# Moving the shares of a triangular inverse in a chunked attention kernel: from nine to seventeen, one behind each dense half unit

## The chip, the cores and the metric

The kernel runs on one core of one Trainium2 chip. The metric is device microseconds of one launch. A core has a matrix engine (PE, with its weight loads PEld), three elementwise engines (DVE, ACT, POOL) that each work through their own list of instructions strictly in order, and SP, which here only starts DMAs. An instruction that needs another engine's result waits for a semaphore, and all that stands behind it on its own engine waits with it.

## What is computed

An attention recurrence over 768 steps, a dense two-layer network on its output, and a layer of eight experts of which each token uses one:

```python
for t in range(S):                                   # r,k,v,w,a,b: (4, 8, 768, 40)
    y[:, :, t] = einsum('bhd,bhde->bhe', r_t, state)
    Sa = einsum('bhde,bhe->bhd', state, a_t)
    state = state * w_t[:, :, None, :] - einsum('bhd,bhe->bhde', Sa, b_t) + einsum('bhd,bhe->bhde', v_t, k_t)
x = y.transpose(0, 2, 1, 3).reshape(3072, 320)
h = x @ w_in                                         # 320 -> 2048
x = maximum(0.01 * h, h) @ w_out                     # 2048 -> 320
e = argmax(x @ w_gate)                               # 8 experts
out = softmax(x @ w_gate)[e] * (relu(x @ w1[e]) @ w2[e])
```

## The kernel before, in words

**Attention in chunks.** The 768 steps are cut into 24 chunks of 32. Inside a chunk the recurrence becomes a triangular system. The kernel prepares a chunk some six chunks ahead in fifteen steps (`prep`): clamp and scans of the decay on DVE (L216, L224, L226, L239), two reciprocals (L232, L233), a product on POOL (L231, tile `AtI`), the keys on POOL and DVE (L242, L243, tile `KB`), small matmuls (L265), masks and copies, and at last DMAs, of which one kind collects the triangular blocks of four chunks in the tile `Pq` (L287). When four chunks are prepared, `inverse` turns `Pq` into the inverses of all their triangles at once. It has 62 steps: the first is a transpose on DVE from `Pq` into `Tinv` (L301); then come thirty pairs on POOL, a product into `itmp` (L309) and a sum into `Tinv` (L315), where each needs the one before; the last is a copy (L321) and a transpose (L323) on DVE into `TT`. The chunk's own steps s1 to s6 read `TT` in s2 (matmuls of L414), the first time in the chunk three after the one in which the inverse began. The inverses that this case is about begin in chunks 5, 9, 13 and 17 and have to be there in chunks 8, 12, 16 and 20.

**The dense layer runs beside it**, since the attention of an earlier pair of chunks is its input. It goes in units, each of 128 of the 2048 hidden columns for 256 tokens, and each unit in two half units. The first half issues layer 1: eight matmuls into a bank of PSUM (L722), then `g` on ACT (L726) and DVE (L727), then `gh`, the rounded `g`, on ACT (L728). The second half issues the six matmuls of layer 2 for the unit two back (L738; they need that unit's `gh`, and last its `gl`), and then `gl = g - gh` on POOL (L729) for this unit. There are two buffers of `g`, two PSUM banks for layer 1, and three of `gh` and `gl`. So ACT may only write `g` of a unit when POOL has made `gl` of the unit two before, and PE may only finish layer 2 of a unit when POOL has made its `gl`. Beside both stand the gate's logits of the tokens that are done (DVE L762, tile `junk`).

**The order is written by hand.** Each chunk plays a string of words: `H` is a half unit, `p` the next step of the preparation, `s1` to `s6` the chunk's own steps, `l2` and `l3` loads, and `w` a share of the inverse. A share takes the next steps of the open inverse, and how many follows from what is left and from how many shares are still to come up to the end of the third chunk:

```python
turns, k = order.count("w"), 0          # shares in this chunk's string
...
elif what == "w":
    for _ in range(-(-len(inv) // (turns * (4 - here % 4) - k))):
        inv.pop(0)()
    k += 1
```

`here` is the chunk's number. `len(inv)` is rounded up in the division, and in a chunk with number 4n+1 the divisor holds the chunk's full count of shares, also those that were played before the inverse was there. `STEP` is the string of chunks 5 to 18, `LATE` of 19 to 22, and both are at the top of the file. The preparation ends in chunk 17, so chunk 18 has the inverse and no preparation beside it.

Of the kernel before, what the change touches and what calls it, by code (L numbers as in the profile page):

```python
# [22 lines left out]
B, H, S, D = 4, 8, 768, 40  # L23
# [27 lines left out]
)  # L51
STEP = (
    "w s6a.-1 s1 s6b.-1 H H H s2 H H p w p p s3a s3x H l2.1 H p w p w p w p w p s3b p H H s4a p p s4b H p H w s5a s5b H p H p H w H w p H l3.1 "
)
LATE = (
    "s6a.-1 H H s1 H s6b.-1 w s2 H H w s3a s3x H w H s3b H l2.1 H H w H w s4a w s4b H s5a s5b H w H H w H l3.1 H w "
)
END = (
    "H H s1 H s2 w w H H H w H s6a.-1 s6b.-1 w s3x H H s3a w H s4a s4b H w H s5a s5b w l3.1 H H s3b H l2.1 H H w w H "
# [1417 lines left out]
```

## Time and profile before

| what | us |
|---|---|
| median of 3 runs (1087.32 to 1091.97) | 1090.9 |
| the profiled execution's own time | 1100.18 |
| its span | 1098.4 |
| PE busy | 929.3 |
| DVE busy | 807.6 |
| ACT busy | 531.3 |
| POOL busy | 512.3 |

The profiled execution is 9.3 us above the median of the runs. Its span is the time from its first to its last instruction, and 1.8 us lie around it. The busy times are sums over the whole program; what an engine does in one chunk is seen only in a window of that chunk. In the rows below a chunk is taken from its first matmul of s1 (L399) to the next chunk's.

### The profile page before, as it was taken

What the parts mean: (1) busy time and instruction counts of PE and PEld (TensorE: products, weight loads), DVE (VectorE), ACT (ScalarE), POOL (GpSimd) and SP (SyncE); (2) the same over time, 40 slices, a digit from 0 to 9 for tenths busy, and PEclk for the clock granted to TensorE, in tenths of its full rate; (3) what the DMA queues carried; (4) which work ended last, traced back from release to release, by engine and by line L of the source; (5) the groups of instructions that cost most, each with busy time, mean ns of one, the idle gap of its engine ahead of it and who ended that gap; (6) DMA issues with size and microseconds to landing.
All of it is one profiled execution on the core that took longest, in us unless ns stands there. A gap on an engine that the chain in (4) does not pass through costs nothing.

```text
span 1098.4 us, 40672 instructions
## 1 busy us (share of the span) xinstructions
PE 929.3 (85%) x16854; PEld 871.4 (79%) x16854; DVE 807.6 (74%) x1900; ACT 531.3 (48%) x1316; POOL 512.3 (47%) x690
## 2 busy tenths in 40 slices
PE   2265778878799888889889998999999799999995
PEld 1255667777788878878779887998899699999995
DVE  8988788866778786868787666567656777877771
ACT  3545554663334444444435443444446466666661
POOL 5124145215873399447964585333556432332221
PEclk9999986888889999999999998999999899999998
DMA  7878876856546555575656442332425537354440
GB/s 250 228 213 228 227 208 178 232 149 172 151 114 173 140 162 159 141 169 138 158 151 144 124 78 73 91 82 55 151 90 140 204 129 246 100 169 146 140 126 16
DMA packets 143991, 166.04 MB, mean 151 GB/s; under 512 B 67931, under 2 KB 105451, under 8 KB 143671
## 3 DMA queue, kind: packets, MB, share of 16 engines
q1 hardware_dynamic: 133687, 144.20, 47.9%
q10 hardware_dynamic: 5760, 10.49, 3.3%
q0 software_dynamic: 4352, 8.69, 2.5%
q8 instruction: 134, 2.20, 0.9%
q14 instruction: 58, 0.48, 0.2%
HBM read 127.62 MB, written 42.27 MB: 155 GB/s over the span
## 4 chain that ended last, share of the span: by engine, by line
PE 42%; DVE 24%; DMA 9%; issue 9%; POOL 8%; ACT 6%; SPq 1%; POOLq 0%; DVEq 0%; ACTq 0%
PE psH L722 9%; PE psX L738 8%; PE epy L1162 8%; PE psH L1146 6%; DVE junk L762 3%; PE eph L1146 3%; DVE g L727 2%; POOL itmp L309 2%; POOL Tinv L315 2%; DMA L<-dKBr 2%; PE psA L414 2%; POOL gl L729 2%; DVE lam L226 1%; PE psA L486 1%; DVE Rr L472 1%
## 5 line engine op out<-in xcount | busy, mean ns | idle before, releaser
L729 POOL TENSOR_TENSOR gl<-g,gh 128x256 fp32r<-128x256 f32 x192 | 156.9, 820 | 221.4 <-ACT gh L728 186.7
L727 DVE TENSOR_TENSOR g<-psH,g 128x256 f32<-128x256 f32 x192 | 81.2, 423 | 108.2 <-ACT g L726 97.3
L728 ACT CAST gh<-g 128x256 fp32r<-128x256 f32 x192 | 78.2, 407 | 163.6 <-DVE g L727 156.7
L738 PE MATMUL psX<-woh,gh 128*128 128x320 f32 x384 | 134.0, 349 | 1.3 <-ACT woh L649 1.1
L738 PE MATMUL psX<-woh,gl 128*128 128x320 f32 x384 | 124.9, 325 | 6.9 <-POOL gl L729 6.6
L726 ACT ACTIVATE g<-psH 128x256 f32<-128x256 f32 x192 | 73.8, 384 | 109.0 <-PE psH L722 89.6
L738 PE MATMUL psX<-wol,gh 128*128 128x320 f32 x384 | 123.3, 321 | 0.0
L762 DVE SCALAR_TENSOR_TENSOR junk<-X,raws 128x320 bf16<-128x320 f32 x160 | 93.3, 583 | 4.6 <-ACT X L759 2.7
L722 PE MATMUL psH<-xh,wih 128*128 128x256 f32 x384 | 87.4, 311 | 4.9 <-DVE g L727 4.0
L309 POOL TENSOR_TENSOR itmp<-Tinv 128x30 f32<-128x30 f32 (+14 forms) x120 | 72.8, 607 | 33.9 <-DVE Tinv L301 26.7
L738 PEld LDWEIGHTS psX<-woh,gl 128*128 128x128 f32 x384 | 76.3, 199 | 10.2 <-POOL gl L729 9.7
L722 PE MATMUL psH<-xl,wih 128*128 128x256 f32 x384 | 81.3, 295 | 0.0
L722 PE MATMUL psH<-xh,wil 128*128 128x256 f32 x384 | 80.9, 294 | 0.0
L738 PEld LDWEIGHTS psX<-woh,gh 128*128 128x128 f32 x384 | 76.3, 199 | 5.4 <-ACT woh L649 1.3
L265 PE MATMUL psA<-AtI,KB 40*64 40x72 f32 x1408 | 43.9, 264 | 42.3 <-DVE KB L243 18.9
L1174 POOL DMA_INDIRECT out<-ey,sid x32 | 33.3, 1041 | 97.2 <-ACT ey L1173 91.7
L315 POOL TENSOR_TENSOR Tinv<-Tinv,itmp 128x30 f32<-128x30 f32 (+14 forms) x120 | 73.7, 614 | 7.8
L738 PEld LDWEIGHTS psX<-wol,gh 128*128 128x128 f32 x384 | 76.8, 200 | 0.3 <-DVE wol L650 0.3
L265 PEld LDWEIGHTS psA<-AtI,KB 40*64 40x64 f32 x1408 | 35.5, 163 | 49.7 <-POOL woh L242 18.3
L722 PEld LDWEIGHTS psH<-xh,wih 128*128 128x128 f32 x384 | 66.3, 201 | 10.1 <-DVE g L727 6.5
L1150 DVE SCALAR_TENSOR_TENSOR ehl<-psH,ehh 128x256 fp32r<-128x256 f32 x86 | 36.2, 421 | 41.5 <-ACT ehh L1149 38.6
L722 PEld LDWEIGHTS psH<-xl,wih 128*128 128x128 f32 x384 | 63.6, 203 | 0.3 <-DVE xl L707 0.3
(292 smaller groups left out, 2775.5 us busy)
## 6 DMA issues: line engine op xcount, KB each, us to landing
raw<-hwe SPq DMA_DIRECT2D x48, 512.0 KB
raw<-hwe SPq DMA_DIRECT2D x32, 640.0 KB
in<-h SPq DMA_DIRECT2D x23, 521.0 KB
KB<-h SPq DMA_DIRECT2D x22, 512.0 KB
L<-dKBr SPq DMA_DIRECT2D x24, 320.0 KB
dKBr<-KBr SPq DMA_DIRECT2D x22, 320.0 KB
lamY<-dl SPq DMA_DIRECT2D x24, 264.0 KB
dl<-lam SPq DMA_DIRECT2D x22, 264.0 KB
```

The source lines that it names most:

```text
L265: nc.tensor.matmul(box[i][64 * j:64 * j + 64, k, :], z["KB"][o, p, :], z["AtI"][o, p, :], start=True, stop=True)
L309: eng.tensor_tensor(out=box["v"], in0=T[:, k + 1:32, k:k + 1].to_broadcast([128, n, k]), in1=T[:, k:k + 1, 0:k].to_broadcast([128, n, k]), ...
L315: eng.tensor_tensor(out=T[:, k + 1:32, 0:k], in0=T[:, k + 1:32, 0:k], in1=box["v"], op=ALU.add)
L722: nc.tensor.matmul(ps[:, 0:256], w, x, start=(n == 0), stop=(n == 7))
L726: nc.scalar.activation(out=g, in_=ps[:, 0:256], func=AF.Copy, scale=0.01)
L727: nc.vector.tensor_tensor(out=g, in0=ps[:, 0:256], in1=g, op=ALU.max)
L728: nc.scalar.copy(out=gh, in_=g)
L729: return gh, gl, lambda: nc.gpsimd.tensor_tensor(out=gl, in0=g, in1=gh, op=ALU.subtract)
L738: nc.tensor.matmul(s.x2[t][:, 0:DM], x[:, o], w[:, f, :], start=(f == 0 and n == 0), stop=(f == NF - 1 and n == 2))
L762: nc.vector.scalar_tensor_tensor(out=s.junk, in0=X[:, t, 0:DM], scalar=1.0, in1=s.wg[:, e], op0=ALU.mult, op1=ALU.mult, accum_out=lg[:, t, ...
L1146: nc.tensor.matmul(ps, w, x, start=(n == 0), stop=(n == 7))
L1162: nc.tensor.matmul(s.y[t][:, 0:DM], x[:, o], w, start=(f == 0 and n == 0), stop=(f == 7 and n == 2))
```

## The change

Only the two strings change. A share stands behind each half unit from the third word of the chunk on. `STEP` has 17 shares where it had 9, `LATE` likewise. Without the `w` each string reads word for word as before, so nothing else is moved in what the program issues.

```diff
 STEP = (
-    "w s6a.-1 s1 s6b.-1 H H H s2 H H p w p p s3a s3x H l2.1 H p w p w p w p w p s3b p H H s4a p p s4b H p H w s5a s5b H p H p H w H w p H l3.1 "
+    "s6a.-1 s1 s6b.-1 H w H w H w s2 H w H w p p p s3a s3x H w l2.1 H w p p p w p p s3b p H w H w s4a p p s4b H w p H w s5a s5b H w p H w p H w H w p H w l3.1 "
 )
 LATE = (
-    "s6a.-1 H H s1 H s6b.-1 w s2 H H w s3a s3x H w H s3b H l2.1 H H w H w s4a w s4b H s5a s5b H w H H w H l3.1 H w "
+    "s6a.-1 H w H w s1 H w s6b.-1 s2 H w H w s3a s3x H w H w s3b H w l2.1 H w H w H w s4a s4b H w s5a s5b H w H w H w H w l3.1 H w "
 )
```

By the formula a share holds three steps of the inverse before, throughout. After, it holds two until twenty steps are left, and then one. POOL gets of an inverse's sixty products and sums:

| chunk of the three | before | after |
|---|---|---|
| first (5, 9, 13, 17) | 8 | 13 |
| second (6, 10, 14, 18) | 27 | 31 |
| third (7, 11, 15, 19) | 25 | 16 |

The lists of PE, SP and ACT are the same before and after. The first place is POOL in the second chunk of an inverse (here chunk 6; chunks 10 and 14 are alike). Before, four shares stand with only steps of the preparation between them:

```order
L729 TENSOR_TENSOR gl<-g,gh 128x256
L309 TENSOR_TENSOR itmp<-Tinv 128x184
L315 TENSOR_TENSOR Tinv<-Tinv,itmp 128x23x8
L309 TENSOR_TENSOR itmp<-Tinv 128x198
L315 TENSOR_TENSOR Tinv<-Tinv,itmp 128x22x9
L309 TENSOR_TENSOR itmp<-Tinv 128x210
L315 TENSOR_TENSOR Tinv<-Tinv,itmp 128x21x10
L309 TENSOR_TENSOR itmp<-Tinv 128x220
L315 TENSOR_TENSOR Tinv<-Tinv,itmp 128x20x11
L309 TENSOR_TENSOR itmp<-Tinv 128x228
L315 TENSOR_TENSOR Tinv<-Tinv,itmp 128x19x12
L309 TENSOR_TENSOR itmp<-Tinv 128x234
```

After, in the same engine and place:

```order
L729 TENSOR_TENSOR gl<-g,gh 128x256
L315 TENSOR_TENSOR Tinv<-Tinv,itmp 128x23x8
L309 TENSOR_TENSOR itmp<-Tinv 128x198
L315 TENSOR_TENSOR Tinv<-Tinv,itmp 128x22x9
L309 TENSOR_TENSOR itmp<-Tinv 128x210
L729 TENSOR_TENSOR gl<-g,gh 128x256
L315 TENSOR_TENSOR Tinv<-Tinv,itmp 128x21x10
L309 TENSOR_TENSOR itmp<-Tinv 128x220
L315 TENSOR_TENSOR Tinv<-Tinv,itmp 128x20x11
L309 TENSOR_TENSOR itmp<-Tinv 128x228
L729 TENSOR_TENSOR gl<-g,gh 128x256
```

Where up to twelve products and sums stood between two `gl`, there are four, and four between every two `gl` all through the chunk.

The second place is DVE in chunk 5, where the inverse begins (chunks 9, 13 and 17 are alike, with a logit more or less between); the difference of the two lists, with `-` before and `+` after:

```order
 L472 TENSOR_TENSOR Rr<-psA,mask 64x256 x2
 L762 SCALAR_TENSOR_TENSOR junk,lg<-X_3991,raws 128x320
+L301 STREAM_TRANSPOSE Tinv<-Pq 128x1024
 L232 RECIPROCAL d1r<-lam 128x15
 L233 RECIPROCAL d1r<-lam 128x1
 L727 TENSOR_TENSOR g<-psH,g 128x256
 L762 SCALAR_TENSOR_TENSOR junk,lg<-X_3991,raws 128x320
-L301 STREAM_TRANSPOSE Tinv<-Pq 128x1024
 L493 TENSOR_TENSOR Y<-psA,lamY 40x512 x2
 L762 SCALAR_TENSOR_TENSOR junk,lg<-X_3991,raws 128x320
```

The transpose, which waits for the DMA into `Pq`, now stands ahead of a unit's `g`. At the inverse's end the copy and transpose into `TT` come one logit later in chunks 8, 12 and 16.

## Rows read from the trace of the kernel before

**Rows 1.** Page: engines' busy time; then groups: busy, mean ns of one | idle before.

```profile
PE 929.3 (85%) x16854; PEld 871.4 (79%) x16854; DVE 807.6 (74%) x1900; ACT 531.3 (48%) x1316; POOL 512.3 (47%) x690
...
L729 POOL TENSOR_TENSOR gl<-g,gh 128x256 fp32r<-128x256 f32 x192 | 156.9, 820 | 221.4 <-ACT gh L728 186.7
...
L728 ACT CAST gh<-g 128x256 fp32r<-128x256 f32 x192 | 78.2, 407 | 163.6 <-DVE g L727 156.7
```

**Rows 2.** Chunks 10, 11, 12, 14, 18: stretch, length, PE, PEld, DVE, ACT, POOL, PEclk, DMA.

```profile
382.71:412.79 30.08, 25.82 (x588) 23.37 (x586) 26.51 (x68) 13.21 (x36) 28.35 (x38) 1.00 0.58 154
412.79:442.46 29.67, 26.81 (x582) 24.61 (x581) 21.08 (x47) 12.67 (x33) 26.29 (x39) 0.94 0.55 150
442.46:470.69 28.23, 25.34 (x588) 23.33 (x586) 25.25 (x68) 12.86 (x35) 11.62 (x16) 1.00 0.59 162
501.85:531.38 29.53, 25.53 (x587) 23.23 (x586) 26.18 (x68) 13.21 (x36) 27.81 (x38) 1.00 0.58 156
...
617.69:644.39 26.70, 25.38 (x537) 23.64 (x535) 18.64 (x52) 11.27 (x29) 23.81 (x39) 1.00 0.40 101
```

**Rows 3.** Waits of the whole program: engine, line, releaser; us in total, times, longest.

```profile
ACT g L726 <- POOL gl L729: 15.8, 12, 2.8
...
PE psX L738 <- POOL gl L729: 6.6, 6, 1.5
```

**Rows 4.** Timeline of PE: five of those six waits, [idle before <- releaser].

```profile
411.44 0.41 PE L738 MATMUL psX<-woh,gl 128*128 128x320 f32 x1 [1.52 <-POOL gl L729]
437.26 0.42 PE L738 MATMUL psX<-woh,gl 128*128 128x320 f32 x1 [1.05 <-POOL gl L729]
530.02 0.42 PE L738 MATMUL psX<-woh,gl 128*128 128x320 f32 x1 [1.50 <-POOL gl L729]
537.89 0.41 PE L738 MATMUL psX<-woh,gl 128*128 128x320 f32 x1 [0.96 <-POOL gl L729]
637.33 0.42 PE L738 MATMUL psX<-woh,gl 128*128 128x320 f32 x1 [1.23 <-POOL gl L729]
```

**Rows 5.** Windows of POOL, tile `Tinv` alone: five stretches of the second inverse.

```profile
379.60:388.30 8.70, 3.63 (x8) 1.00 0.61 137
388.80:393.72 4.92, 3.23 (x5) 1.00 0.59 156
393.72:418.00 24.28, 15.57 (x22) 0.93 0.60 167
418.50:430.03 11.53, 6.54 (x9) 1.00 0.46 119
430.03:447.00 16.97, 8.94 (x16) 1.00 0.50 142
```

**Rows 6.** Timeline of chunk 12, without an inverse: POOL's `gl`, PE's use of it.

```profile
470.69 1.19 POOL L729 TENSOR_TENSOR gl<-g,gh 128x256 fp32r<-128x256 f32 x1
...
473.21 0.31 PE L738 MATMUL psX<-woh,gl 128*128 128x320 f32 x1
```

**Rows 7.** Timeline where an inverse begins: DVE and PE in chunk 5, DVE in chunk 9.

```profile
247.71 0.42 DVE L727 TENSOR_TENSOR g<-psH,g 128x256 f32<-128x256 f32 x1
251.61 2.00 DVE L301 STREAM_TRANSPOSE Tinv<-Pq 128x1024 f32<-128x1024 f32 x1 [3.07 <-DMA Pq<-Ms]
...
255.05 0.41 PE L738 MATMUL psX<-woh,gl 128*128 128x320 f32 x1
...
376.75 0.43 DVE L727 TENSOR_TENSOR g<-psH,g 128x256 f32<-128x256 f32 x1 [1.84 <-ACT g L726]
```

**Rows 8.** Timeline of ACT in chunk 7.

```profile
297.25 0.39 ACT L726 ACTIVATE g<-psH 128x256 f32<-128x256 f32 x1 [1.86 <-POOL gl L729]
```

**Rows 9.** Windows behind three waits; columns as in rows 2, PEclk third from the end.

```profile
297.70:307.90 10.20, 6.64 (x150) 6.01 (x154) 1.93 (x5) 2.03 (x6) 6.70 (x10) 0.50 0.50 117
...
413.80:417.20 3.40, 3.40 (x19) 3.32 (x17) 0.51 (x3) 1.15 (x4) 3.06 (x5) 0.50 1.09 247
530.10:533.50 3.40, 3.40 (x97) 3.12 (x98) 1.47 (x5) 2.17 (x6) 3.32 (x4) 1.00 0.85 199
```

## The prediction

> **What bounds the kernel now.** I read the page's busy times first [rows 1]: PE is busy 85% of the span and POOL, which does the inverse, 47%. By these shares POOL's order would hardly matter. So I read the windows of single chunks [rows 2]. Chunk 12 has no inverse: 28.23 us, of which PE is busy 25.34 and POOL 11.62. Chunk 10 is the second of the three chunks over which an inverse is spread, and there POOL is busy 28.35 of 30.08 us with 38 instructions; the 1.73 us left is 0.046 us behind each instruction. POOL is full from end to end there, and the chunk is 30.08 - 28.23 = 1.85 us longer than chunk 12. Chunk 14 is the same case: 27.81 of 29.53, 1.30 longer.
>
> The waits show how a full POOL reaches PE [rows 3]: PE's layer 2 (L738) waits for `gl` six times, 6.6 us in all, and ACT's `g` (L726) waits for `gl` to free its buffer twelve times, 15.8 us. The single PE waits [rows 4] lie in chunks 10, 11, 14, 15 and 18: 1.52, 1.05, 1.50, 0.96 and 1.23 us. ACT is busy 48%, so most of its waits cost nothing; one that may is that of 1.86 us in chunk 7 [rows 8].
>
> A second cost can hang on such waits. After the wait that ends at 411.44, PE's granted clock is 0.50 (1.2 GHz) from 413.80 to 417.20; after the like wait at 530.02 it stays at 1.00 (2.4 GHz) [rows 4, 9]. Chunk 11 shows the price of the first: PE is busy 26.81 us there, against 25.34 in chunk 12, for nearly as many matmuls: 1.47 us [rows 2].
>
> **What the change does, part by part.** PE, ACT and SP keep their order. What moves is when POOL does sixty instructions four times over, and a few DVE instructions.
>
> *Second chunks (10, 14, 18; and 6).* The change does two opposite things. It breaks up the burst: twelve products and sums between two `gl` become four. But since shares of two steps, rounded up, are now seventeen a chunk, the second chunk gets 31 instead of 27. They are also costlier ones: summing the five stretches of the second inverse [rows 5], the second chunk's 27 cost 3.23 + 15.57 = 18.80 us (numbers 9 to 35), and numbers 14 to 44, which it has after, 15.57 + 6.54 = 22.11. So +3.31 us on an engine that is full. Chunk 10 then wants 28.35 + 3.31 + 42 x 0.046 = 33.6 us of POOL, against 28.23 that it would need without an inverse: 5.4 over. Some of this PE doesn't feel, since a `gl` has time to spare: in chunk 12 one ends at 470.69 + 1.19 = 471.88 and is used at 473.21, 1.3 us later [rows 6]. With 1.3 to spare the chunk loses 4.1 us, with twice that (some units have more) 2.8; it now loses 1.85. That is +0.9 to +2.2; I take +1.5. If nothing is to spare it is 33.6 - 30.08 = +3.5, and with 4 us to spare -0.4: these are the ends. Chunk 14 by the same steps wants 27.81 + 3.31 + 1.9 = 33.0, 4.8 over, so 2.2 to 3.5 of loss where it has 1.30: again +0.9 to +2.2, taken +1.5. Chunk 18 has no preparation and fewer `gl`: 23.81 + 3.3 + (39 + 4) x 0.046 = 29.1 us of POOL, and without its wait the chunk takes 26.70 - 1.23 = 25.5. That is 3.6 over, less 1.3 to 2.6, so 1.0 to 2.3 against 1.23 now; I take +1.0, since with so little other POOL work the backlog builds up in fewer units, and +2.4 and -0.2 as ends. In chunk 6 the work for s2 is longer and POOL was not full, so nothing.
>
> *Third chunks (11, 15, 19; and 7).* They get 16 products and sums instead of 25, 8.94 us instead of 6.54 + 8.94 = 15.48 [rows 5]. The waits of 1.05 and 0.96 at 437.26 and 537.89 [rows 4] should go. But in chunk 11 PE idles 29.67 - 26.81 = 2.86 us and in chunk 12 2.89 [rows 2], so part of such a wait only takes another's place. I take -0.7 each, with -1.05 and 0 as ends. In chunk 7 the 1.86 us that ACT waits [rows 8] should go too; I take -1.0 (ends 0 and -1.9). Chunk 19 has no wait of PE in rows 4, so nothing.
>
> *First chunks (5, 9, 13, 17).* They get 13 instead of 8, 6.86 us against 3.63 [rows 5], while POOL is half idle: nothing, covered by that idle time. The transpose L301 moves ahead of a unit's `g` on DVE. In chunk 5 it waits for the DMA into `Pq` until 251.61, and `g`, which ran at 247.71 before it [rows 7], now queues behind: 251.61 + 2.00 + 0.42 gives 254.0 for `g` (with the two reciprocals between, 254.4), `gh` adds 0.41 and `gl` 0.82 [rows 1], with their hops about 256.2, and PE's layer 2 wants this `gl` at 255.05 [rows 7]. About +1.5 us; 0 and +2 are the ends. In chunks 9, 13 and 17 the `Pq` DMA is not what the transpose waits for, and in chunk 9 DVE idles 1.84 us before `g` comes [rows 7], alike in the others, which the transpose's 2.0 us now fills: nothing, covered; if that cover fails, some 0.5 each.
>
> *The end of the inverse* comes in the same chunk, with the copy and transpose into `TT` one logit later in DVE's list. Its steps come off POOL sooner than before, so nothing.
>
> The sum is 1.5 + 1.5 + 1.0 - 1.4 - 1.0 + 1.5 = **+3.1 us**, and no change of the clock is in it. Made on the profiled execution, 1100.18 becomes 1103.3; on the median of the runs, 1090.9 becomes 1094.0.
>
> **A rule on the clock that speaks against the change.** The trace shows 1.47 us lost in chunk 11 after one wait of 1.52 us and nothing after another of 1.50 [rows 2, 4, 9]. The Trainium skill, "TensorE: Matmul & The Clock Gate", section "HAM oscillation — how this bites in real kernels", says that waits between groups of matmuls let the clock fall, so that each group starts slow. By that rule the longer waits of chunks 14 and 18 would each bring such a stretch: +1.5 each, and the sum would be +6.1, so 1097. The trace bears it out in one of the two waits. I leave it out of the sum, since I expect the waits spread over several units, and have it at the forecast's upper end and in the slower rival.
>
> **Rivals.**
> - *Faster: breaking the burst is what counts.* If spare time in the units is 4 us or more, POOL at four steps a unit just keeps up. Then all waits of PE for `gl` go (-6.6 [rows 3]), chunk 7's (-1.0) and the slow stretch in chunk 11 (-1.5), against +1.5 in chunk 5: -7.6, so 1083. It decides itself at the unit: a `gl` and four steps cost POOL about 0.82 + 4 x (22.11 / 31 + 0.046) = 3.86 us, a unit of chunk 12 28.23 / 8 = 3.53, and over eight units 2.6 us of spare time would have to be there, beside `AtI` and `KB`. Against it: chunk 10 already shows 1.85 us lost with less work. The slow stretch of 10.2 us in chunk 7 [rows 9], if it shrank with ACT's wait, would give up to 3 more.
> - *No change: the losses only change places.* Second chunks lose what third chunks give back, and chunk 5's transpose hides: 0 to +1.5, so 1091 to 1092.4. This and the forecast differ only in sizes.
> - *Slower: POOL's backlog counts in full.* A `gl` that comes late holds not only PE's layer 2 but ACT's next `g`, and with it what stands behind on ACT, so that the 1.3 us of rows 6 are used up before PE's wait shows. Then chunks 10, 14 and 18 take POOL's time whole: +3.5, 33.0 - 29.53 = +3.5, and +2.4, together 9.4 in place of the 4.0 of the sum: +8.5, so 1099.4, and with one or two stretches at 1.2 GHz at 1.5 each 1101 to 1102.4. It decides itself at spare times under half a microsecond. For it: chunk 10 is now as long as POOL's time, 30.08, with nothing to spare. Against it: rows 6.
> - *The change doesn't do what it says:* it speaks of small even shares, and the formula makes them two, two, ..., one. The forecast has this in it; if the text were taken at its word (20 steps a chunk) the first rival would be likely.
>
> **How the numbers follow.** The forecast (+1.5 to +6 us) gets 0.45, no change in places (-1.5 to +1.5) 0.15, POOL's backlog in full 0.25, faster 0.15. A measurement of this kernel can tell about 0.5%, 5.45 us, from no change. The forecast lies inside it but for its upper end (0.1 of its 0.45). So faster 0.14, same 0.51, slower 0.35. For the range: at the low end it takes in half of the faster rival, at the high end the backlog in full with a stretch or two at 1.2 GHz: 1085 to 1102.
>
> **What would show it.** Right: in the windows of chunks 10 and 14 POOL busy about 32 us of a chunk of 31 to 32, with PE waiting for `gl` in three or four units by 0.5 to 1.7 us each, in place of one of 1.5; chunks 11 and 15 without such a wait, POOL busy about 19; chunk 18 about 27.7; in chunk 5 `g` at about 254 and PE waiting a microsecond or more for `gl` near 255. Wrong: chunks 10 and 14 of 29 us or less (then units have more to spare than I took), chunks over 33 us, new stretches at 1.2 GHz after chunk 10, or a change in chunks 20 and later, where no share has work.

## The result and the profile after

The changed kernel takes 1102.23 us (median of 5 runs, 1098.48 to 1106.79), the kernel before 1090.9 (5 runs, 1087.32 to 1093.89). The ratio is 1.0109, with an interval of 1.0078 to 1.0140: slower by 1.1%, where the forecast was 1094, +0.3%, with a range that ended at 1102.

Two corrections ahead. The words on the formula say that its divisor also holds shares that were played before the inverse was there. It doesn't: `k` takes them off. It is the rounding up alone that makes 62 steps over 41 shares two, two, ..., one. And the words on the change say that four steps stand between every two `gl` all through the second chunk. In one place it is six, where three shares stand between two half units that end in a `gl`.

The profiled execution of before (1100.18 us) is a long one. A second trace of the same code, `e0_before` below, has a span of 1091.5 and is used beside it. The time of chunks 5 to 19, from the first matmul of s1 of chunk 5 to that of chunk 20, in windows of before, of its second trace, and of after (stretch, length, busy time of PE, PEld, DVE, ACT, POOL, granted clock, DMA share, GB/s):

```profile
215.53:675.96 460.43, 401.58 (x9016) 370.87 (x9014) 343.60 (x847) 197.43 (x520) 286.00 (x401) 0.94 0.55 143
```

```profile
216.56:670.79 454.23, 405.57 (x9015) 376.81 (x9013) 343.43 (x847) 197.28 (x520) 284.87 (x401) 0.92 0.54 145
```

```profile
218.73:679.40 460.67, 403.44 (x9016) 372.57 (x9014) 345.87 (x847) 196.77 (x520) 286.38 (x401) 0.94 0.54 143
```

Two executions of one kernel differ here by 6 us, as much as the change moves one of them. So single traces show where time goes, and medians how much. The mean clock of these stretches is no lower after (0.94) than before (0.94, 0.92). By kind of chunk, summed from such windows:

| chunks | before | its second trace | after |
|---|---|---|---|
| first (5, 9, 13, 17) | 129.1 | 125.4 | 125.0 |
| second (6, 10, 14, 18) | 120.9 | 120.1 | 135.7 |
| third (7, 11, 15, 19) | 126.1 | 129.5 | 116.2 |
| without inverse (8, 12, 16) | 84.3 | 79.2 | 83.7 |

The second chunks lose 15 us and the third ones give back 10 to 13. The second figure is loose: `e3_turn_later` below, with the same steps in these chunks, has 135.7 and 121.3, which is 5 to 8 given back. Chunks 10, 11, 14 and 18 after, which answer to [rows 2]:

```profile
384.27:419.09 34.82, 27.13 (x588) 24.12 (x586) 27.54 (x69) 13.43 (x36) 32.86 (x45) 0.96 0.58 154
419.09:447.42 28.33, 27.46 (x582) 25.75 (x581) 20.48 (x47) 13.21 (x34) 20.39 (x31) 0.87 0.49 133
...
504.52:538.21 33.69, 27.31 (x588) 24.91 (x586) 27.19 (x68) 13.20 (x36) 31.81 (x43) 0.95 0.56 154
...
619.91:651.66 31.75, 26.97 (x537) 23.88 (x535) 19.95 (x58) 11.72 (x31) 29.56 (x47) 1.00 0.35 91
```

In chunk 10 POOL's 32.86 us of work and some 2 us of gaps between 45 instructions are the chunk's 34.82 us: POOL works from end to end, as it did, only with seven instructions more (five and eight more in chunks 14 and 18). The table of the change had four more. Where the second inverse's products and sums really ran is seen in windows of POOL, tile `Tinv` alone, for chunks 9 to 12: length, busy time (number), clock, DMA share, GB/s; first before, then after. A number counts an instruction that lies across a boundary twice.

```profile
353.59:382.71 29.12, 0.52 (x2) 0.94 0.64 156
382.71:412.79 30.08, 18.08 (x27) 1.00 0.58 154
412.79:442.46 29.67, 17.54 (x27) 0.94 0.55 150
442.46:470.69 28.23, 1.78 (x4) 1.00 0.59 162
```

```profile
355.89:384.27 28.38, 3.23 (x7) 0.94 0.65 159
384.27:419.09 34.82, 24.51 (x35) 0.96 0.58 154
419.09:447.42 28.33, 8.98 (x18) 0.87 0.49 133
447.42:475.67 28.25, 1.06 (x2) 0.94 0.59 161
```

The table gives chunks 9 and 10 8 and 27 steps before, 13 and 31 after. So at the start of chunk 10 POOL is six steps behind this count in both kernels (8 - 2, 13 - 7). At its end it is six behind before, and three after: counted by their starts, 27 steps run in chunk 10 before and 34 after. Of the seven more, four are the table's, and three are steps that ran in chunk 11 before.

The waits for `gl` in the whole program, which answer to [rows 3] (15.8 and 6.6 us there; 22.6 and 9.1 in the second trace):

```profile
ACT g L726 <- POOL gl L729: 26.2, 17, 3.1
...
PE psX L738 <- POOL gl L729: 12.1, 12, 3.6
```

The burst is gone, as the lists said, but POOL doesn't rest between two `gl`. Its timeline in chunk 10, with no idle time shown in any row; between two `gl` lie six steps here, since two of the three shares stand with only preparation between:

```profile
400.50 0.98 POOL L729 TENSOR_TENSOR gl<-g,gh 128x256 fp32r<-128x256 f32 x1
401.44 0.68 POOL L315 TENSOR_TENSOR Tinv<-Tinv,itmp 128x228 f32<-128x228 f32 x1
402.19 0.61 POOL L309 TENSOR_TENSOR itmp<-Tinv 128x234 f32<-128x234 f32 x1
402.89 0.79 POOL L315 TENSOR_TENSOR Tinv<-Tinv,itmp 128x234 f32<-128x234 f32 x1
403.75 0.68 POOL L309 TENSOR_TENSOR itmp<-Tinv 128x238 f32<-128x238 f32 x1
404.51 0.71 POOL L315 TENSOR_TENSOR Tinv<-Tinv,itmp 128x238 f32<-128x238 f32 x1
405.30 1.65 POOL L309 TENSOR_TENSOR itmp<-Tinv 128x240 f32<-128x240 f32 x1
406.92 0.72 POOL L729 TENSOR_TENSOR gl<-g,gh 128x256 fp32r<-128x256 f32 x1
```

ACT and PE pay for it one behind the other. ACT's `g` in chunk 10 (three rows, each with its wait), and PE's longest wait for `gl`, which answers to the 1.52 us of [rows 4]:

```profile
401.51 0.38 ACT L726 ACTIVATE g<-psH 128x256 f32<-128x256 f32 x1 [1.88 <-POOL gl L729]
...
411.14 0.39 ACT L726 ACTIVATE g<-psH 128x256 f32<-128x256 f32 x1 [1.23 <-POOL gl L729]
...
416.88 0.38 ACT L726 ACTIVATE g<-psH 128x256 f32<-128x256 f32 x1 [3.07 <-POOL gl L729]
```

```profile
416.90 0.63 PE L738 MATMUL psX<-woh,gl 128*128 128x320 f32 x1 [3.64 <-POOL gl L729]
```

In chunk 10 PE waits 4.4 us in all for `gl`, where it was 1.9, and 2.4 us for DVE's `Rr` (L472), where it was 1.4.

### The profile page after: what moved, and what is told of

The parts are those of the page before. It is cut to its first block, busy times and chain, and to the rows that moved or that the text cites. A ratio compares the mean times of both kernels' runs of the same rounds, so it can differ in the third digit from the quotient of the medians.

```text
span 1100.4 us, 40672 instructions
## 1 busy us (share of the span) xinstructions
PE 932.4 (85%) x16854; PEld 873.6 (79%) x16854; DVE 808.6 (73%) x1900; ACT 529.8 (48%) x1316; POOL 512.6 (47%) x690
## 4 chain that ended last, share of the span: by engine, by line
PE 45%; DVE 22%; POOL 9%; DMA 8%; issue 8%; ACT 6%; SPq 0%; POOLq 0%; DVEq 0%; ACTq 0%
PE psH L722 9%; PE psX L738 9%; PE epy L1162 8%; PE psH L1146 6%; POOL itmp L309 3%; PE eph L1146 3%; POOL Tinv L315 3%; PE psA L414 2%; DVE g L727 2%; POOL gl L729 2%; DVE junk L762 2%; PE psA L486 1%; PE psA L439 1%; DVE Rr L472 1%; DVE lam L226 1%
## 5 line engine op out<-in xcount | busy, mean ns | idle before, releaser
L738 PE MATMUL psX<-woh,gl 128*128 128x320 f32 x384 | 125.2, 326 | 12.3 <-POOL gl L729 12.1
L315 POOL TENSOR_TENSOR Tinv<-Tinv,itmp 128x30 f32<-128x30 f32 (+14 forms) x120 | 77.1, 643 | 4.0
```

What stands on the lines that cost most here:

```text
L315: eng.tensor_tensor(out=T[:, k + 1:32, 0:k], in0=T[:, k + 1:32, 0:k], in1=box["v"], op=ALU.add)
L738: nc.tensor.matmul(s.x2[t][:, 0:DM], x[:, o], w[:, f, :], start=(f == 0 and n == 0), stop=(f == NF - 1 and n == 2))
```

## The experiments

Theory A: POOL's time sets the second chunks, and rounding up gives them too many steps. Its rivals: the seventeen places themselves cost (B); the transpose ahead of `g` costs (C). Each ratio is to 17 to 29 runs of the kernel before that were taken beside the experiment.

**e0_before**, no edit.

> The kernel before once more, for a second trace of it. Both theories: 1.000 of itself, within 0.004; chunks 10, 14 and 18 take about 30, 29.5 and 26.7 us. What it is for: the profiled execution of before took 1100.18 us, 9 us over its median, and I expect this one to be shorter by some of the stretches at 1.2 GHz, not by the waits for gl.

Ratio 0.9994 (0.9971 to 1.0017). Chunk 10 took 28.84 us and chunk 11 32.33 (30.08 and 29.67 in the first trace): PE's waits for `gl` fell in chunk 11 here, where 1.52 us of them stood in chunk 10 in the first trace. The expected lower share of stretches at 1.2 GHz was not there: its mean clock in chunks 5 to 19 is 0.92 against 0.94, and it is shorter all the same.

**e1_even**, the same seventeen places with rounding to the nearest:

```diff
-                for _ in range(-(-len(inv) // (turns * (4 - here % 4) - k))):
+                for _ in range(int(len(inv) / (turns * (4 - here % 4) - k) + 0.5)):
```

> The changed kernel's seventeen shares, but the steps of a share rounded to the nearest whole number instead of up: about 1.5 a share throughout, ten, 26 and 26 steps in the three chunks (before: 9, 27, 26; after: 14, 31, 17). Theory A (what costs is that rounding up loads POOL with 31 steps in the second chunk): no backlog, three steps between two gl, chunks 10 and 14 of 28.3 to 29.5 us, the time 1083 to 1092, ratio 0.993 to 1.001. Theory B (what costs is a share behind every half unit, wherever the steps lie): 1098 to 1104, ratio 1.007 to 1.013.

1088.45 us, ratio 0.9915 (0.9880 to 0.9949): A, against B. In the new places, with 26 steps instead of 31 in the second chunk (and 11 and 25 in the others, not the ten and 26 of the expectation), the loss is gone and turned into a gain, a larger one than expected. Chunks 10, 11 and 14, and PE's waits for `gl` in the whole program:

```profile
382.65:410.59 27.94, 25.49 (x587) 23.26 (x585) 24.78 (x64) 12.16 (x33) 26.77 (x35) 1.00 0.59 163
410.59:442.15 31.56, 26.98 (x582) 24.52 (x580) 26.94 (x59) 14.12 (x37) 29.87 (x40) 0.93 0.61 151
499.00:525.30 26.30, 25.03 (x588) 23.35 (x586) 23.18 (x62) 11.69 (x32) 25.12 (x34) 1.00 0.60 173
...
PE psX L738 <- POOL gl L729: 5.3, 7, 1.8
```

POOL still works without a break in chunks 10 and 14: the 1.2 us that are left are the gaps between its 35 and 34 instructions. But the chunks are no longer than one without an inverse (28.23 and 25.98 us in the two traces of before), and PE waits less than half as much as in the changed kernel. So a POOL without a break doesn't by itself make a chunk longer; what counts, it seems, is whether its list asks for more than PE's units take. The longest of the three is now chunk 11, the third chunk.

**e2_nine_front**, the nine old places with the changed kernel's counts:

```diff
-                for _ in range(-(-len(inv) // (turns * (4 - here % 4) - k))):
-                    inv.pop(0)()
+                if not inv:
+                    size[:] = [5, 5, 4] + [4, 3, 4, 3, 4, 3, 4, 3, 3] + [2] * 8 + [1]
+                else:
+                    for _ in range(size.pop(0)):
+                        inv.pop(0)()
```

> The kernel before with its nine shares where they stand, only their sizes changed so that the three chunks get the changed kernel's 14, 31 and 17 steps (5, 5, 4; 4, 3, 4, 3, 4, 3, 4, 3, 3; 2 eight times and 1). Theory A (31 steps in the second chunk on a full POOL): chunks 10 and 14 of 32.5 to 34.5 us, the time 1097 to 1104, ratio 1.006 to 1.013. Theory B (seventeen places): 1088 to 1094, ratio 0.997 to 1.003.

1109.57 us, ratio 1.0134 (1.0104 to 1.0165): A again, and beyond what was expected. Chunk 10:

```profile
383.70:419.32 35.62, 29.82 (x587) 27.22 (x585) 26.06 (x69) 13.52 (x36) 33.34 (x46) 0.86 0.51 144
```

With before, after and the even shares this makes a square, all beside runs of before within 2.4 us of each other. The columns go by the second chunk; the counts of the other two go along (9 and 26, or 11 and 25, against 14 and 17):

| | 26 or 27 steps in the second chunk | 31 steps |
|---|---|---|
| nine places, with bursts | 1093.23 | 1109.57 |
| seventeen places | 1088.45 | 1102.23 |

The count costs 14 to 16 us, and breaking up the burst gives back 5 to 7. Both of the forecast's opposite effects are real; it is their sizes that were wrong.

**e3_turn_later**: the first share of an inverse is skipped and played with the next one (four steps).

```diff
-                for _ in range(-(-len(inv) // (turns * (4 - here % 4) - k))):
+                n = -(-len(inv) // (turns * (4 - here % 4) - k))
+                if len(inv) == 62:
+                    late.append(n)
+                    n = sum(late) if len(late) == 2 else 0
+                else:
+                    late.clear()
+                for _ in range(n):
```

> The changed kernel, but the inverse's first share is held back until the next share, which then plays both (four steps), so that the transpose stands behind the reciprocals and the unit's g on DVE as before; from then on all is as in the changed kernel. Theory A: chunk 5 gives back 1 to 2 us, chunks 10 and 14 stay at 33 to 35, the time 1099 to 1103, ratio to before 1.007 to 1.012. Theory C (the transpose that waits ahead of g is the cause): chunk 5 and the chunks behind it give back nearly all, 1090 to 1094, ratio 0.999 to 1.003.

1102.49 us, ratio 1.0079 (1.0052 to 1.0106), and chunk 10 as in the changed kernel (35.25 us against 34.82): C falls.

```profile
380.08:415.33 35.25, 28.18 (x588) 25.55 (x586) 25.97 (x68) 13.44 (x36) 33.21 (x46) 0.90 0.56 150
```

In chunk 5 the changed kernel shows the mechanism that the forecast named, and e3 shows it undone: `g` behind the transpose and the wait for `Pq`, and PE's wait at the end of it (after, DVE and PE), against the old order (e3, DVE).

```profile
254.88 2.06 DVE L301 STREAM_TRANSPOSE Tinv<-Pq 128x1024 f32<-128x1024 f32 x1 [4.53 <-DMA Pq<-Ms]
...
257.13 0.42 DVE L727 TENSOR_TENSOR g<-psH,g 128x256 f32<-128x256 f32 x1
...
259.99 0.41 PE L738 MATMUL psX<-woh,gl 128*128 128x320 f32 x1 [0.87 <-POOL gl L729]
```

```profile
249.00 0.42 DVE L727 TENSOR_TENSOR g<-psH,g 128x256 f32<-128x256 f32 x1
...
252.96 2.01 DVE L301 STREAM_TRANSPOSE Tinv<-Pq 128x1024 f32<-128x1024 f32 x1 [3.13 <-DMA Pq<-Ms]
```

Its price of about a microsecond (chunk 5 takes 41.32 us in e3 and 42.48 in the changed kernel) is below what single traces or the medians can tell: the two traces of before have 40.74 and 42.34.

**e4_short_after** and **e5_short_before**: POOL's time taken away, instructions and order kept.

```diff
-                    out=box["v"], in0=T[:, k + 1:32, k:k + 1].to_broadcast([128, n, k]),
-                    in1=T[:, k:k + 1, 0:k].to_broadcast([128, n, k]), op=ALU.mult)
+                    out=box["v"][:, 0:1], in0=T[:, k + 1:k + 2, k:k + 1].to_broadcast([128, 1, k]),
+                    in1=T[:, k:k + 1, 0:k], op=ALU.mult)
...
-                eng.tensor_tensor(out=T[:, k + 1:32, 0:k], in0=T[:, k + 1:32, 0:k], in1=box["v"], op=ALU.add)
+                eng.tensor_tensor(out=T[:, k + 1:k + 2, 0:k], in0=T[:, k + 1:k + 2, 0:k], in1=box["v"][:, 0:1], op=ALU.add)
```

> The changed kernel with each of the sixty products and sums of an inverse cut to its first row (at most 30 elements a partition in place of up to 240); the other rows are left out of the computation, the instructions, their order and their waits stay. Theory A (POOL's time in the second chunk): POOL falls to about 0.3 us an instruction, chunks 10 and 14 to 26 to 28.5 us, the time to 1074 to 1086, and it is level with the next kernel to within 0.4%. Theory B (where the shares stand costs, by the waits and by what is queued): it stays 0.7% or more above the next kernel.

> The kernel before with the same cut to the first row; the other rows are left out. Theory A: 1074 to 1086 as well. Theory B: 1075 to 1080 while the kernel ahead stays 8 us or more above.

1083.10 us, ratio 0.9906 (0.9872 to 0.9940), and 1082.52, ratio 0.9893 (0.9850 to 0.9935): level. Chunks 5 to 19 of the one and of the other:

```profile
216.00:655.30 439.30, 398.85 (x9016) 371.02 (x9014) 329.30 (x847) 195.77 (x520) 215.84 (x401) 0.93 0.57 150
```

```profile
219.35:658.55 439.20, 398.17 (x9015) 371.25 (x9013) 326.24 (x847) 195.65 (x520) 204.75 (x401) 0.94 0.58 150
```

With short steps it doesn't matter, within about half a per cent, where the shares stand, so most of what the change costs, if not all, goes through the length of POOL's steps. DVE's busy time falls along with POOL's, though none of its instructions was changed: 345.87 to 329.30 us in the changed kernel, 343.60 to 326.24 in the one before. So the two runs don't tell POOL's own time from what its work may add to DVE's instructions beside it. They also give an estimate of what any order of the shares can bring: about 9 us below before.

**e6_first_heavy**, seventeen places with a list of sizes as in e2: `[3, 3, 3, 3, 4, 4, 4]`, then 20 steps, then 18.

> The changed kernel's seventeen shares with other sizes: 24 steps in the first chunk (3, 3, 3, 3, 4, 4, 4), 20 in the second, 18 in the third. Theory A: the first chunk's POOL has room (it was busy 10.6 of 29.1 us), the second and third are no longer full, POOL busy 24 to 26 in chunks 10 and 11: 1079 to 1087, ratio 0.987 to 0.995, better than the even shares or level with them. Theory E (the first chunk cannot take 24 steps since the inverse begins in its second half only): chunk 9 grows by 1 to 3 us and the time is 1088 to 1094.

1112.16 us, ratio 1.0163 (1.0124 to 1.0203). This is the miss that teaches most: its list has the fewest steps in the second chunk, and it is the slowest of all. Chunk 9, chunk 10, and POOL where the inverse begins:

```profile
361.80:390.63 28.83, 25.91 (x582) 24.20 (x580) 21.59 (x52) 13.31 (x34) 13.90 (x19) 0.94 0.66 160
```

```profile
390.63:423.23 32.60, 28.14 (x587) 25.86 (x585) 22.54 (x61) 11.76 (x31) 30.80 (x44) 0.90 0.48 137
```

```profile
378.52 0.85 POOL L729 TENSOR_TENSOR gl<-g,gh 128x256 fp32r<-128x256 f32 x1 [2.55 <-ACT gh L728]
384.56 0.25 POOL L309 TENSOR_TENSOR itmp<-Tinv 128x30 f32<-128x30 f32 x1 [5.18 <-DVE Tinv L301]
...
387.67 1.68 POOL L729 TENSOR_TENSOR gl<-g,gh 128x256 fp32r<-128x256 f32 x1
389.32 0.60 POOL L315 TENSOR_TENSOR Tinv<-Tinv,itmp 128x84 f32<-128x84 f32 x1
...
394.42 0.73 POOL L729 TENSOR_TENSOR gl<-g,gh 128x256 fp32r<-128x256 f32 x1
```

POOL was busy only 13.90 us of chunk 9, but the idle time lies ahead of the transpose: the first product comes at 384.56, six us before the chunk ends. Only seven of the 23 products and sums that the first chunk's string lists are done in it, and 32 run in chunk 10, where the list has 20. What stands in the first chunk's string behind that point is done in the second's time, and here with up to eight steps between two `gl`, 6.75 us from one to the next where a unit of PE takes some 3.5. Theory E had the place right (the inverse begins late) and the chunk wrong: not chunk 9 grew but chunk 10. The excess over the changed kernel lies elsewhere: its second chunks take 133.8 us (135.7 there), the first ones 129.4 (125.0) and the third ones 125.8 (116.2).

**e7_two_first** (14, 24, 24), **e9_second_28** (14, 28, 20) and **e10_last_heavy** (7, 28, 27), lists of sizes in the seventeen places.

> The same seventeen shares with 14 steps in the first chunk (as in the changed kernel), 24 in the second and 24 in the third. Theory A: a step less in the full third chunk than the even shares: 1084 to 1089, ratio 0.991 to 0.997; with the changed kernel (31 in the second) and the first-heavy one (20) it gives the price of a step. Theory B: as the changed kernel, 1098 or more.

> Seventeen shares with 14, 28 and 20 steps, between 14, 24, 24 (ratio 0.997) and the changed kernel's 14, 31, 17 (1.011). Theory A with a price for each step from the start of a full POOL: ratio 1.004 to 1.008, chunk 10 of 30 to 32 us. If there is a threshold of spare time that four more steps do not use up: 0.995 to 1.000.

> Seventeen shares with 7, 28 and 27 steps, one step a share at the start. By the count in the second chunk alone it is the kernel ahead: ratio 1.003 to 1.008. If the backlog is built from the start of the inverse on, over the stretch from the end of the first chunk (what I think since 24, 20, 18 was 1.016): fewer steps before the second chunk pay for those in it, 0.992 to 0.999.

Ratios 0.9968 (0.9945 to 0.9991), 1.0011 (0.9991 to 1.0031) and 0.9990 (0.9969 to 1.0010). e7's 1090.31 us lie a little above what was expected. e9 and e10 have the same count in the second chunk and differ by seven steps ahead of it, yet they are level; and e9 came out between the two expectations, its chunk 10 at 28.85 us and not at 30 to 32. Ordered by the steps that are to be done up to the end of the second chunk:

| kernel | steps up to there | ratio to before |
|---|---|---|
| e10 | 35 | 0.9990 |
| e1 | 37 | 0.9915 |
| e7 | 38 | 0.9968 |
| e9 | 42 | 1.0011 |
| e6 | 44 | 1.0163 |
| after | 45 | 1.0109 |

Up to 42 the ratios lie between 0.9915 and 1.0011, and with two or three steps more at 1.011 to 1.016. That looks less like one price for each step than like a point from which POOL no longer keeps up, but it is not shown: the counts of the third chunk change along, e1 and e12 below, with the same counts (and other buffers), lie 0.7% apart, and e6 lies above the changed kernel with a step less. In chunk 10 of e9 POOL works without a break too, and the chunk is as short as before's 28.84 and 30.08 us.

```profile
385.44:414.29 28.85, 25.62 (x587) 23.25 (x585) 25.70 (x63) 12.11 (x33) 27.52 (x36) 1.00 0.57 157
```

**e8_even_keys_dve**, the even shares (with e1's edit) and two of POOL's products on DVE in the third chunks:

```diff
     for c in range(5, NC):
+        at.mul = nc.vector if c % 4 == 3 else nc.gpsimd
```

> The even shares (ratio 0.9915) with POOL's two products of the preparation, AtI (L231) and half of KB (L242), on DVE in the third chunks 7, 11 and 15, where the even shares left POOL 29.9 of 31.6 us busy and chunk 11 at 31.6 us. Theory A (POOL is what is full there): chunks 11 and 15 fall by 1.5 to 3 us each, the time 1079 to 1086, ratio 0.984 to 0.991. Rival F (DVE, 25 to 27 us busy there, passes the delay on through g): 1087 to 1093, ratio 0.991 to 0.998.

1089.62 us, ratio 0.9956 (0.9928 to 0.9985): no gain over e1, whose interval it overlaps, inside what rival F expected and outside Theory A's range. Chunk 11 took 30.72 us (31.56 in e1) and chunk 15 stayed at 31.84 with POOL at 29.62. But the edit took less off POOL there than meant: the product of `KB` that chunk 11's string lists ran in e1 only at 442.2 us, in chunk 12, so that of the two only `AtI`'s 1.2 us left chunk 11. Whether DVE passes the delay on, as F has it, is not shown.

**e11_three_g** and **e12_even_three_g**: three buffers of `g` and two of `gl`.

```diff
-        g = s.p2.tile([128, 256], F32, name="g", tag="g")
+        g = s.p3.tile([128, 256], F32, name="g", tag="g")
...
-        gl = s.p3.tile([128, 256], F32R, name="gl", tag="gl")
+        gl = []
+
+        def close():
+            gl.append(s.p2.tile([128, 256], F32R, name="gl", tag="gl"))
+            nc.gpsimd.tensor_tensor(out=gl[0], in0=g, in1=gh, op=ALU.subtract)
...
```

> The changed kernel with three buffers of g and two of gl in place of two and three (gl's buffer is taken only when POOL writes it), so that ACT's g waits for the gl of the unit three before instead of two. Theory A1 (what I subtracted as spare time is not there since a late gl holds ACT's next g, and through it the next gl: a ring): ACT's waits for gl fall from 26 us to under 12, the second chunks give back 1 to 2 us each, the time 1094 to 1099, ratio to before 1.001 to 1.006. Theory A2 (POOL's plain throughput sets the second chunks, whatever the buffers): ACT's waits fall but PE's waits for gl grow by as much, 1099 to 1104, ratio 1.007 to 1.013.

> The even shares (ratio 0.9915) with the same buffers. Theory A1: the third chunks 11 and 15, 31.5 us with even shares, fall by 1 to 2 us each, 1080 to 1086, ratio 0.985 to 0.991. Theory A2: as the even shares, ratio 0.990 to 0.995.

1106.16 us, ratio 1.0149 (1.0118 to 1.0181), and 1087.96, ratio 0.9985 (0.9961 to 1.0010). In e11 the waits change sides (the lines have moved by five):

```profile
PE psX L743 <- POOL gl L729: 18.9, 19, 2.4
...
ACT g L731 <- POOL gl L729: 7.2, 9, 1.6
```

ACT's fall from 26.2 us to 7.2, PE's grow from 12.1 to 18.9, and chunk 10 stays at 34.58 us. That is A2's pattern, though slower than A2's range: POOL's throughput, not the ring through `g`'s buffers. (Two buffers of `gl` hold POOL up elsewhere, 82 us of waits for PE in the whole program; in chunk 10 no gap of POOL is longer than 0.08 us.) e12 brought nothing over e1, and its ratio lies above both expectations; 1088.45, 1089.62 and 1087.96 are the medians of the three even kernels, their ratios 0.9915 to 0.9985. So the even shares beat the changed kernel by 1.2 to 1.9%. The kernel before they beat clearly in e1 and e8, by 0.9 and 0.4%; in e12 the interval takes in no difference.

## Why the prediction was wrong

**What held.** The bound (POOL at work without a break in chunks 10 and 14), the rounding up that puts 31 steps in the second chunk, the two opposite effects, chunk 5's wait (0.87 us of PE against the 1.5 taken, `g` at 257.1 where the DMA came 3.3 us later than in the first trace), chunk 11 without PE's wait, and no change in chunks 20 and later. The outcome is the rival "POOL's backlog counts in full", for which 1099.4 to 1102.4 was worked out. It had been given 0.25. That it meets the total of 1102.23 is in part luck: it had the second chunks at +9.4 and the third at -2.4, and the windows show other parts (below). Two of the signs of being wrong came: chunks 10 and 14 took over 33 us, and stretches at 1.2 GHz stand behind chunk 10's and chunk 14's waits.

**The step that failed: spare time.** From POOL's excess of 5.4, 4.8 and 3.6 us in chunks 10, 14 and 18 the working took off 1.3 to 2.6 us each, since in chunk 12 a `gl` ends 1.3 us ahead of its use [rows 6]. But chunk 12 is a chunk in which POOL is idle 60% of the time. In chunk 10 the reserve was used up before the change: PE waits 1.52 us for `gl` at its end [rows 4], and by the same subtraction the kernel before would lose 1.85 - 1.3 = 0.55 us there, where the prediction itself has 1.85. What is used up can't be taken off a second time. The row against it stood in the prediction ("with nothing to spare") and was given less weight than a row from another stage. In its place the runs show the steps counting in full: e2 and e1 put the price of the counts at 14 to 16 us, e4 and e5 show that most of it goes through the length of POOL's steps, and e11's third buffer of `g` didn't mend it.

**The term of +3.31 us, mis-sized.** The prediction prices by the table: four steps more in chunk 10, 3.31 us. In the windows above POOL spends 24.51 us on the inverse there in place of 18.08, seven steps more. The first chunks are not the reason: 13 steps instead of 8 were costed at nothing there, and that held, since POOL comes out of chunk 9 six steps behind the table in both kernels (the first product starts at 379.0 and 379.6 us, though in the changed kernel's chunk 9 DVE's transpose waits 0.97 us for the DMA into `Pq`, where none was forecast). Four of the seven are the table's, and the other three ran in chunk 11 before. e6 shows where such room ends: of 23 steps listed in the first chunk only seven fit in behind the inverse's input.

**The sizes.** Second chunks: +4.0 forecast, about +15 measured (+4.7 to +6.0, +4.2 and +5.0 in chunks 10, 14 and 18, +0.5 to +0.9 in chunk 6). Third chunks: -2.4 forecast, -10 to -13 measured (-5 to -8 in e3). Part of both is the same work on the other side of a boundary: counted in all four inverses, nine steps now run in the second chunks that ran in the third before; at 0.72 us each (24.51 / 34) they are some 6 us, an estimate. Without them the second chunks lose 8 to 9, near the rival's 9.4. For the third chunks only the single waits of PE [rows 4] had been counted; that a POOL which comes out of chunk 10 late and still has 25 steps holds up ACT and DVE in chunk 11 too is argued, not shown. The two errors have opposite signs; by the medians the change costs 11.3 us where 3.1 was forecast, 8 more.

**The clock.** In the last 0.7 us of the wait of 3.64 us the granted clock falls to 0.50 (1.2 GHz), for 10.2 us, 2.9 of them in chunk 10 and 7.3 in chunk 11:

```profile
416.20:426.40 10.20, 9.50 (x119) 8.81 (x122) 3.63 (x12) 3.59 (x8) 9.26 (x14) 0.50 0.65 166
```

Behind the wait of 2.92 us at the end of chunk 14 stands a stretch of 3.4 us (539.06 to 542.46), and behind chunk 18's waits of 1.36 and 1.28 none. The rule of the Trainium skill ("TensorE: Matmul & The Clock Gate", section "HAM oscillation — how this bites in real kernels") that waits between matmuls let the clock fall is borne out for the longer waits. But chunk 11 with that stretch is no longer than before (28.33 us against 29.67 and 32.33), and PE's idle time there is 0.87 us where it was 2.86 in the first trace: it seems to have taken up the slower matmuls. Over the runs the changed kernel's mean clock is a little lower, 0.951 against 0.953 to 0.955 in the four sets of runs of before that stand beside the experiments. Among the executions of one kernel, 0.01 less of mean clock goes with some 2.8 us more (a line fitted through all 206 on record, each kernel by itself). By that, an estimate, the clock makes about 1 us of the 11. It is not where most of them went.

**What stays open.** How the loss splits between ACT's waits and PE's over the whole program; whether there is a point from which POOL no longer keeps up, and where; why chunks 12 and 16 take 26 us in one execution and 28.2 in another of the same kernel (chunk 12 in both traces of before at a granted clock of 1.00); and why e6's first and third chunks are longer than the changed kernel's (more steps between two `gl` at the start is argued, not shown).

## What to carry to other kernels

Where one engine's busy time and its small gaps add up to the length of a stage, and others already wait for it there, count each microsecond added to its list as a microsecond of the stage: take off no reserve that was read in another stage. Without such waits the sum alone says little, as e1's chunks 10 and 14 show. Where an engine lags behind its list, count what runs in a stage by its own window, not by the list. Room on an engine counts only behind the input that its work waits for, so read the idle time by what ends it, not by its sum. When work is cut into more shares, work out how many steps each share gets: rounding up turned an even spread into a front-loaded one, and rounding to the nearest (e1) made the same seventeen shares faster than both.

## What the runs showed that was not expected

- In the same seventeen places, 31 steps in the second chunk take 1102.23 us and 26 take 1088.45.
- An engine can work through a chunk without a break and the chunk be as short as one without that work: e1's chunk 14, 26.30 us.
- All sixty of POOL's instructions cut to a row each, which takes 80 us of its busy time in four inverses (286 to 205 in chunks 5 to 19), bring only 9 us: in the kernel before POOL's steps hold the rest up by little.
- A third buffer moved 19 us of waits away from ACT and none of it off the end.
